# Splitting the first three 256-token passes of an FFN into chunks, with other decode points and lags

## The chip, the cores and the metric

The kernel runs on one core of a Trainium2 chip. The metric is device microseconds of one execution. The core's engines are PE (TensorE, the matrix engine), DVE (VectorE), ACT (ScalarE), POOL (GpSimd) and SP (SyncE, which issues all DMAs here). Each runs its own instructions strictly in the order in which they stand in its stream; semaphores make one engine wait for another.

## The reference, cut to what matters

```python
# q, k, v: (4, 8, 576, 64); windowed causal attention with a distance bias
scores = q @ k.T / 8 + bias, masked to 0 <= i - j < 128
attn   = softmax(scores);  x = (attn @ v)  -> (2304, 512)
x = ((x @ w_a) * (x @ w_b)) @ w_out         # FFN 1: 512 -> 1536 -> 512
h = x @ w_in                                # FFN 2: 512 -> 2048 -> 512
g = where(h >= 1, h, where(h <= -1, 0, (h + 1)**2 / 4))
return g @ w_out2
```

The weights arrive as 64-bit floating point numbers. The kernel turns each 512x128 or 128x512 piece into two 32-bit pieces, `wh` and `wl` (high and low part), and each product of the FFNs is made of three matmuls: `wh*xh`, `wh*xl` and `wl*xh`.

## The kernel before, in words

**Attention.** `attention()` is a generator: every `next` of it (a *step*, made by `step()`) emits one of three things for a round (batch, head pair, pair of 64-query blocks): `scores` (matmuls `ps_s`, L316; bias, mask and row maximum on DVE, L322; exponential on ACT, L326; scaling by the row sum on POOL and ACT), `transposes` (matmuls `ps_t`, L352, of the softmaxed tile `s`), or `values` (matmuls `ps_o`, L377, which use 64 of PE's columns each). The transposes of a round come `LT` = 3 rounds after its scores, its values `LV` = 5 rounds after. A round has one or two *strips*, one DVE instruction L322 each, 144 in all; strips are used as a clock below. In the program's order one `ps_o` instruction is two records of the trace.

**Weights.** `pump()` takes the next weight piece in the order a0, b0, o0, a1, ... (a and b feed the gate of slice f, o its way back), and `decode` emits its load and its conversion: on DVE L471, L474, L475, L476, L478, on ACT L468 and L485, on POOL (for the first 15 pieces) L484 and L142 `wl`. There are 15 slots for pieces, enough for slices 0 to 4, and 2 more once attention is over. A slot comes free when its piece has been used for the last time. Before attention's end pieces are pumped at every second step made while the next half of tokens is being waited for, or when a product asks for a piece that isn't there; the first `HPN` pieces are emitted at high priority.

**FFN 1.** Tokens are cut in nine *halves* of 256 and in five blocks of 512 (the last of 256). While attention runs, FFN 1 goes half by half: for half i and slice f, `gate` makes 24 matmuls into `mm` tiles (L519 to L521, 256 columns wide), then `down1_half` 12 into two `acc` tiles (L592); at the end of a half the `acc` tiles are copied to `y` and written to a DRAM buffer `x2p`. Halves 0 and 1 take slices 0 to 3, the others 0 to 4 (`N0`). After that FFN 1 goes by blocks of 512 columns for slices up to 8 and then up to 11 (`down1`, L620 to L622), starting from what `x2p` holds. FFN 2 follows (L652 to L654). I call all `mm` and `acc` matmuls *FFN matmuls*.

**What sets the order.** `products()` yields after every three matmuls, and each yield earns `PACE` steps of attention (0.8 in the first two halves, then 0.5); before a half begins, steps are made until its tokens are `ready`. The resulting program is then reordered within each engine by a scheduler that works from priorities and its own timeline, so where an instruction stands must be read from the order it made.

Of the kernel before, what the change touches and what calls it, by code (L numbers as in the profile page):

```python
# [9 lines left out]
F32 = mybir.dt.float32  # L10
# [4 lines left out]
ALU = mybir.AluOpType  # L15
# [11 lines left out]
def attention_and_two_ffns(  # L27
# [12 lines left out]
    nc = tc.nc  # L40
# [4 lines left out]
    P = 128  # L45
# [4 lines left out]
    TB = 512  # L50
# [7 lines left out]
    halves = [(t, HB) for t in range(0, NT, HB)]  # L58
# [10 lines left out]
    E_X = ['A', 'A', 'A', 'A', 'A', 'A', 'A', 'A']  # L69
    E_Y = 'AV'  # L70
    G2 = [5, 11]
    HPN = 6
    LORD = [['q', 0, 2, True], ['k', 0, 2, True], ['q', 2, 4, False], ['k', 2, 4, False], ['q', 4, 6, False], ['k', 4, 6, False], ['q', 6, 8, False], ['k', 6, 8, False], ['v', 0, 8, 0]]
    LT = 3
    LV = 5
    N0 = [4, 5, 5, 5, 5]
    N1 = 9
    NDIAG = 2
    PACE = [0.8, 0.8, 0.5, 0.5, 0.5, 0.5, 0.5, 0.5, 0.3]
    PT = 3  # L80
    PUMP = [2, 0]
    SB = 4
    TURN1 = [0, 1, 2, 3, 4]
    TURN2 = [4, 0, 1, 2, 3]
# [21 lines left out]
    later = {}  # L106
# [42 lines left out]
        else:  # L149
            ENG[e].tensor_copy(o, i)  # L150

    count = {"t": 0}

# [245 lines left out]
    done = set()  # L401

    def attention():
        load_start()
        prep_unit(0)
        seen = -1
        for n in range(len(todo) + LV):
            if n < len(todo):
                u, t = todo[n]
                if u != seen:  # L410
                    seen = u
                    if u + 1 < len(units):
                        prep_unit(u + 1)
                    if u + AHEAD < len(units):
                        load_unit(*units[u + AHEAD])
                    values_of[units[u]] = load_values(*units[u])
                scores(*t)
                yield
            if 0 <= n - LT < len(todo):
                transposes(*todo[n - LT][1])  # L420
                yield
            if 0 <= n - LV < len(todo):
                values(*todo[n - LV][1])
                done.add(todo[n - LV][1])
                yield

    def ready(t1):
# [103 lines left out]
    def work(name):  # L531
        if later:
            return later["act"].tile([P, TB], F32, tag="t", name=name)
        return act.tile([P, HB], F32, tag="t", name=name)
# [15 lines left out]

    x2p = dram.tile([P, len(halves), NC, HB], F32, name="x2p")
    sums = {}

    def gate(x, f, n, final):

# [24 lines left out]

    def down1_half(i, f, fs, g, final, accs):

        if f == fs[0]:
            accs[:] = [ps_acc.tile([P, TB], F32, tag="acc", name="acc") for _ in range(2)]
        wh, wl = weight(("o", f))
        gh, gl = (z[:, :HB] for z in g)
        for c in range(NC):
            dst = accs[c // 2][:, (c % 2) * HB : (c % 2) * HB + HB]
            cs = slice(c * P, (c + 1) * P)
            opens, closes = f == fs[0] and c % 2 == 0, f == fs[-1] and c % 2 == 1  # L590
            for z, (w, m) in enumerate(((wh, gh), (wh, gl), (wl, gh))):
                nc.tensor.matmul(  # L592
                    dst, w[:, cs], m, start=opens and z == 0, stop=closes and z == 2,
                    skip_group_check=True,
                )
            yield
        if f in final:
            retired.add(("o", f))
        if f == fs[-1]:
            for z in range(2):  # L600
                y = work("y") if later else act.tile([P, TB], F32, tag="y", name="y", bufs=1)
                ecopy(E_Y[z], y, accs[z])
                nc.sync.dma_start(
                    x2p[:, i, 2 * z : 2 * z + 2, :], y.rearrange("p (c t) -> p c t", c=2)
                )
# [64 lines left out]
    def products():  # L670
        behind = deque()

        def run(up, down, i, fs, x, n, final, lag):
            accs = []
            for f in fs:
                g = yield from up(x, f, n, final)
                behind.append(down(i, f, fs, g, final, accs))
                while len(behind) > lag:
                    yield from behind.popleft()
                if later:  # L680
                    pump()

        turns1 = [
            *((i, range(N0[t0 // TB])) for i, (t0, _) in enumerate(halves)),
            *((i, range(N0[i], N1)) for i in TURN1),
            *((i, range(N1, NF1)) for i in TURN2),
        ]
        last = {f: n for n, (_, fs) in enumerate(turns1) for f in fs}
        for n, (i, fs) in enumerate(turns1):
            final = {f for f in fs if last[f] == n}  # L690
            if fs[0] == 0:
                t0, w = halves[i]
                yield t0 + w
                at = t0 % TB
                x = tuple(z[:, :, at : at + HB] for z in xs[t0 // TB])
                yield from run(gate, down1_half, i, fs, x, w, final, 1)
            else:
                yield from run(gate, down1, i, fs, xs[i], blocks[i][1], final, 1)

        turns = [len(blocks) - 1, *range(len(blocks) - 1)]  # L700
        for fs in groups2:
            if fs[-1] == NF2 - 1:
                turns = range(len(blocks))
            for i in turns:
                final = fs if i == turns[-1] else ()
                yield from run(bend, down2, i, fs, xs[i], blocks[i][1], final, 2)
        while behind:
            yield from behind.popleft()


    at = attention()

    def step():
        if later:
            return
        try:
            next(at)
        except StopIteration:
            first.close()
            later["dec"] = ctx.enter_context(tc.tile_pool(name="wdec2", bufs=1))  # L720
            later["act"] = ctx.enter_context(tc.tile_pool(name="act2", bufs=2))
            later["sum"] = ctx.enter_context(tc.tile_pool(name="sums", bufs=1))
            later["g"] = ctx.enter_context(tc.tile_pool(name="g2", bufs=1))
            w2 = ctx.enter_context(tc.tile_pool(name="w2", bufs=W2))
            later["acc"] = ctx.enter_context(tc.tile_pool(name="ps_acc2", bufs=2, space=PSUM))
            later["mm"] = ctx.enter_context(tc.tile_pool(name="ps_mm2", bufs=2, space=PSUM))
            slots.append((w2, W2, deque()))

    steps = 0
    owed = 0.0  # L730
    begun = -1
    for need in products():
        if need is not None:
            begun += 1
            while not later and not ready(need):
                step()
                steps += 1
                if steps % PUMP[0] == PUMP[1]:
                    pump()
        owed += PACE[min(begun, len(PACE) - 1)]  # L740
        while owed >= 1.0:
            owed -= 1.0
            step()
# [30 lines left out]
```

## Time and profile before

| what | value |
|---|---|
| median of 3 runs | 1011.68 us (1011.15 to 1013.41) |
| profiled execution, whole | 1012.14 us |
| its span in the trace | 1010.0 us |
| PE busy | 985.0 us, 98% of the span |
| DVE busy | 619.2 us, 61% |
| ACT busy | 409.2 us, 41% |
| POOL busy | 184.0 us, 18% |

A busy PE is not PE at its peak: matmuls overlap, and the profile counts the time from one's start to its modelled end. To see PE's true pace, take the distance between the starts of two neighbours. "PEclk" is the share of full clock that PE was granted; the engine knows two levels, 1.2 and 2.4 GHz. Idle time counts only on the engine that sets the end of its stage, so the profile is read by stretches.

### The profile page before, as it was taken

To read this page: it belongs to the slowest core of one execution; us is meant where nothing else is said; L and a number is where in the kernel's file an instruction comes from. 1 tells how busy PE (TensorE), PEld (TensorE's weight loads), DVE (VectorE), ACT (ScalarE), POOL (GpSimd) and SP (SyncE) were. 2 spreads that over 40 slices of the span, in tenths; PEclk is the share of its full clock that TensorE was granted. 3 is DMA by queue.
4 is the path that set the end of the run, shared out by engine and by line. 5 is a ranking of instruction groups with operands and counts; after the bars stand their busy time and mean duration, and the time that the engine had idled before them with its cause. 6 is when DMAs were issued, how large, how long until landed. Compare 5 with 4: busy or idle time off the path is not lost.

```text
span 1010.0 us, 15777 instructions
## 1 busy us (share of the span) xinstructions
PE 985.0 (98%) x5804; PEld 849.7 (84%) x5804; DVE 619.2 (61%) x1393; ACT 409.2 (41%) x975; POOL 184.0 (18%) x300
## 2 busy tenths in 40 slices
PE   5989999999999999999999999999999999999998
PEld 4768899999999988888988888888888888888887
DVE  7999644445437898212897279743996446644443
ACT  5877656565424343111343245433552223322222
POOL 5777522222211100000122224000020000000001
PEclk8999999999999999999999999999999999999999
DMA  7757443243053443000232012200231000001111
GB/s 168 152 126 155 95 91 83 48 81 76 1 188 115 151 152 104 1 1 1 65 104 84 0 42 85 63 1 1 66 102 42 1 1 21 1 1 42 43 42 63
DMA packets 136861, 67.10 MB, mean 66 GB/s; under 512 B 107472, under 2 KB 127952, under 8 KB 136272
## 3 DMA queue, kind: packets, MB, share of 16 engines
q1 hardware_dynamic: 136784, 66.09, 24.4%
q8 instruction: 46, 0.75, 0.3%
q14 instruction: 31, 0.25, 0.1%
HBM read 56.62 MB, written 9.44 MB: 65 GB/s over the span
## 4 chain that ended last, share of the span: by engine, by line
PE 87%; DVE 6%; DMA 3%; ACT 2%; issue 1%; POOL 1%; SPq 1%; DVEq 0%; POOLq 0%; ACTq 0%
PE mm L519 16%; PE mm L520 15%; PE mm L521 15%; PE acc L652 7%; PE acc L653 6%; PE acc L654 6%; PE acc L592 6%; PE ps_s L316 3%; PE ps_o L377 3%; PE acc L622 3%; PE acc L620 3%; PE acc L621 3%; PE ps_t L352 2%; DMA kraw<-in_k_dram 2%; DVE e L478 1%
## 5 line engine op out<-in xcount | busy, mean ns | idle before, releaser
L519 PE MATMUL mm<-xh,wh 128*128 128x512 f32 (+1 forms) x952 | 332.0, 350 | 0.2
L521 PE MATMUL mm<-xh,wl 128*128 128x512 f32 (+1 forms) x952 | 321.0, 337 | 0.9 <-POOL wl L142 0.9
L520 PE MATMUL mm<-xl,wh 128*128 128x512 f32 (+1 forms) x952 | 321.3, 338 | 0.0
L519 PEld LDWEIGHTS mm<-xh,wh 128*128 128x128 f32 x952 | 180.0, 189 | 25.0 <-issue 3.6
L521 PEld LDWEIGHTS mm<-xh,wl 128*128 128x128 f32 x952 | 179.9, 189 | 20.4 <-POOL wl L142 1.1
L520 PEld LDWEIGHTS mm<-xl,wh 128*128 128x128 f32 x952 | 180.0, 189 | 19.7 <-issue 0.3
L575 ACT ACTIVATE c_sb<-c_sb,half 128x512 f32<-128x512 f32 (+1 forms) x80 | 54.5, 682 | 165.7 <-DVE c_sb L574 165.7
L652 PE MATMUL acc<-wh,gh 128*128 128x512 f32 x288 | 112.3, 390 | 0.5 <-ACT gh L541 0.5
L653 PE MATMUL acc<-wl,gh 128*128 128x512 f32 x288 | 112.2, 390 | 0.0
L654 PE MATMUL acc<-wh,gl 128*128 128x512 f32 x288 | 110.4, 390 | 0.0
L574 DVE TENSOR_SCALAR c_sb<-mm 128x512 f32<-128x512 f32 (+1 forms) x80 | 50.8, 635 | 81.8 <-PE mm L521 78.9
L564 DVE TENSOR_TENSOR a_sb<-mm,a_sb 128x256 f32<-128x256 f32 (+1 forms) x79 | 40.5, 513 | 93.8 <-PE mm L521 91.3
L142 POOL TENSOR_TENSOR gl<-c_sb,gh 128x256 fp32r<-128x256 f32 x16 | 15.4, 962 | 384.4 <-ACT gh L541 377.8
L326 ACT ACTIVATE s<-s,nmax 128x192 f32<-128x192 f32 (+2 forms) x144 | 62.1, 432 | 54.2 <-DVE nmax L322 53.1
L142 POOL TENSOR_TENSOR gl<-a_sb,gh 128x256 fp32r<-128x256 f32 x50 | 40.3, 806 | 223.0 <-ACT gh L541 222.7
L576 DVE SCALAR_TENSOR_TENSOR c_sb<-mm,c_sb 128x512 f32<-128x512 f32 (+1 forms) x80 | 50.7, 635 | 39.0 <-ACT c_sb L575 39.0
L322 DVE CUSTOM_DVE_ANT_0 s<-ps_s,bias 128x192 f32<-128x192 f32 (+2 forms) x144 | 43.2, 329 | 47.0 <-PE ps_s L316 46.8
L541 ACT CAST gh<-a_sb 128x256 fp32r<-128x256 f32 (+1 forms) x79 | 38.2, 483 | 83.0 <-DVE a_sb L564 82.8
L541 ACT CAST gh<-c_sb 128x512 fp32r<-128x512 f32 (+1 forms) x80 | 46.2, 579 | 56.3 <-DVE c_sb L576 46.3
L468 ACT ACTIVATE e<-w 128x512 f32<-128x512 f32 x65 | 43.9, 675 | 58.4 <-DMA w<-in_moe_w_out_dram 15.1
L485 ACT CAST wh<-e 128x512 fp32r<-128x512 f32 x68 | 42.2, 621 | 59.3 <-DVE e L484 37.4
L559 ACT COPY a_sb<-mm 128x256 f32<-128x256 f32 (+1 forms) x79 | 35.3, 447 | 75.7 <-PE mm L521 73.1
(83 smaller groups left out, 1672.1 us busy)
## 6 DMA issues: line engine op xcount, KB each, us to landing
w<-in_moe_w_out_dram SPq DMA_DIRECT2D x28, 512.0 KB, 3.5
w<-in_moe_w_in_dram SPq DMA_DIRECT2D x16, 512.0 KB, 3.7
w<-in_moe_w_a_dram SPq DMA_DIRECT2D x12, 512.0 KB, 4.3
w<-in_moe_w_b_dram SPq DMA_DIRECT2D x12, 512.0 KB, 4.2
x2p<-y SPq DMA_DIRECT2D x18, 256.0 KB, 2.1
out_dram<-osum SPq DMA_DIRECT2D x18, 256.0 KB, 2.0
xsum<-x2p SPq DMA_DIRECT2D x4, 1024.0 KB, 6.5
kraw<-in_k_dram SPq DMA_DIRECT2D x64, 56.0 KB, 2.5
```

The source lines that it names most:

```text
L142: eng.tensor_tensor(out_, a, hi.bitcast(F32), ALU.subtract)
L326: nc.scalar.activation(at(z, i), at(z, i), AF.Exp, bias=nmax[:, z : z + 1], scale=-1.0, accum_out=ssum[:, z : z + 1],)
L519: nc.tensor.matmul(ps, wh[:, cs], xh[:, c], start=(c == 0), stop=False)
L520: nc.tensor.matmul(ps, wh[:, cs], xl[:, c], start=False, stop=False)
L521: nc.tensor.matmul(ps, wl[:, cs], xh[:, c], start=False, stop=(c == NC - 1))
L541: nc.scalar.copy(hi[:, :n], t[:, :n])
L574: nc.vector.tensor_scalar(c_sb[:, :n], ph[:, :n], -1.0, None, ALU.max)
L575: nc.scalar.activation(c_sb[:, :n], c_sb[:, :n], AF.Square, bias=half, scale=0.5)
L592: nc.tensor.matmul(dst, w[:, cs], m, start=opens and z == 0, stop=closes and z == 2, skip_group_check=True,)
L652: nc.tensor.matmul(accs[s], gh[:, ss], wh, start=begin, stop=False)
L653: nc.tensor.matmul(accs[s], gh[:, ss], wl, start=False, stop=False)
L654: nc.tensor.matmul(accs[s], gl[:, ss], wh, start=False, stop=end)
```

## The change

Twelve passes over halves take the place of nine: halves 0 and 1 first do slices 0 and 1, half 2 slices 0 to 2; then each returns for the rest up to slice 4. All halves now do slices 0 to 4. A returning pass reads its part of `x2p` back into a tile `before`, adds it on DVE to both `acc` tiles and writes the sum. Pieces are pumped at listed step numbers (`PUMP`: 2, 5, 8, then every sixth step up to 194), whoever makes the step. The first `NEARLY` = 8 rounds have lags 2 and 3 in place of 3 and 5. `PACE` is 0.8 for the first six passes, 0.6 for four, then 0.5. Three pieces, not six, have high priority.

```diff
-    HPN = 6
+    HPN = 3
+    EARLY = (2, 3)
+    NEARLY = 8
-    N0 = [4, 5, 5, 5, 5]
+    N0 = 5
+    HALVES = [[0, 0, 2], [1, 0, 2], [2, 0, 3], [0, 2, 5], [1, 2, 5], [2, 3, 5], [3, 0, 5], ...]
-    PACE = [0.8, 0.8, 0.5, 0.5, 0.5, 0.5, 0.5, 0.5, 0.3]
+    PACE = [0.8, 0.8, 0.8, 0.8, 0.8, 0.8, 0.6, 0.6, 0.6, 0.6, 0.5, 0.5]
-    PUMP = [2, 0]
+    PUMP = [2, 5, 8, 14, 20, 26, 32, ..., 188, 194]
...
+        def lag(n):
+            return EARLY if n < NEARLY else (LT, LV)
+        events = sorted(
+            [(n, 0, n) for n in range(len(todo))]
+            + [(n + lag(n)[0], 1, n) for n in range(len(todo))]
+            + [(n + lag(n)[1], 2, n) for n in range(len(todo))]
+        )
...
         if f == fs[0]:
+            if f > 0:
+                before[i] = (later["sum"] if later else act).tile(
+                    [P, 2, TB], F32, tag="before", name="before", bufs=1
+                )
+                nc.sync.dma_start(
+                    before[i].rearrange("p z (c t) -> p (z c) t", c=2), x2p[:, i]
+                )
...
+                if f >= fs[0] > 0:
+                    y = before[i][:, z]
+                    nc.vector.tensor_tensor(y, accs[z], y, ALU.add)
+                    nc.sync.dma_start(
+                        x2p[:, i, 2 * z : 2 * z + 2, :], y.rearrange("p (c t) -> p c t", c=2)
+                    )
+                    continue
...
+        count["step"] += 1
+        if count["step"] in PUMP:
+            pump()
...
-                steps += 1
-                if steps % PUMP[0] == PUMP[1]:
-                    pump()
```

The first place that matters is PE between strips 52 and 64, where all tokens of batch 0 are done and half 2 is being made ready. Before, half 0 and half 1 stand there (`xh_106` is the high part of the tokens of block 0; `s`, `diag`, `kt`, `v` are tiles of attention):

```order
L520 MATMUL mm<-xl_107,wh 128x256
L521 MATMUL mm<-xh_106,wl 128x256
L316 MATMUL ps_s<-kt,diag_130 128x192 x2
L352 MATMUL ps_t<-ident,s_135 128x128 x4
L377 MATMUL ps_o<-pt,v_150 64x128 x2
L519 MATMUL mm<-xh_106,wh 128x256
L520 MATMUL mm<-xl_107,wh 128x256
L521 MATMUL mm<-xh_106,wl 128x256
```

Now, on PE at the same strips, what stands there is attention and the first matmuls of half 2 (`xh_108` is block 1), taken as its tokens appear:

```order
L319 MATMUL ps_s<-kt,diag_130 128x192 x2
L380 MATMUL ps_o<-pt,v_150 64x128 x4
L355 MATMUL ps_t<-ident,s_138 128x128 x4
L319 MATMUL ps_s<-kt,diag_130 128x192
L530 MATMUL mm<-xh_108,wh 128x256 x2
L531 MATMUL mm<-xl_109,wh 128x256
L532 MATMUL mm<-xh_108,wl 128x256
L531 MATMUL mm<-xl_109,wh 128x256
L532 MATMUL mm<-xh_108,wl 128x256
L355 MATMUL ps_t<-ident,s_141 128x128 x2
```

Counted over the whole order: before strip 52's scores stand 110 FFN matmuls before the change and 120 after it; before strip 64's, 235 and 156; before strip 144's, 1005 and 672. In all there are 4668 and 4704.

The second place is PE after strip 64, where every `ps_o` group stood in one run between FFN matmuls:

```order
L592 MATMUL acc<-gl,wh 128x256
L592 MATMUL acc<-gh,wl 128x256
L377 MATMUL ps_o<-pt,v_150 64x128 x4
L592 MATMUL acc<-gh,wh 128x256
```

With the change, on PE, groups there stand in pieces and next to other attention work:

```order
L612 MATMUL acc<-gl,wh 128x256
L380 MATMUL ps_o<-pt,v_146 64x128 x2
L612 MATMUL acc<-gh,wl 128x256
L380 MATMUL ps_o<-pt,v_146 64x128 x2
L319 MATMUL ps_s<-kt,diag_128 128x192 x2
L355 MATMUL ps_t<-ident,s_138 128x128 x4
L380 MATMUL ps_o<-pt,v_146 64x128 x2
L612 MATMUL acc<-gh,wh 128x256
```

After strip 64, 188 `ps_o` instructions stand in 52 unbroken runs before the change and in 65 after it.

## Rows read from the trace of the kernel before

**Rows 1.** The page: busy time, share and instructions of each engine.

```profile
PE 985.0 (98%) x5804; PEld 849.7 (84%) x5804; DVE 619.2 (61%) x1393; ACT 409.2 (41%) x975; POOL 184.0 (18%) x300
```

**Rows 2.** By stretch: length, busy PE, PEld, DVE, ACT, POOL, clock, DMA share, GB/s.

```profile
10.00:83.20 73.20, 61.47 (x477) 50.64 (x478) 67.92 (x229) 57.79 (x192) 53.77 (x77) 0.95 0.67 144
83.20:112.30 29.10, 28.11 (x225) 24.93 (x222) 25.78 (x72) 18.45 (x56) 18.88 (x26) 1.00 0.67 146
112.30:285.00 172.70, 172.70 (x1490) 158.45 (x1489) 79.73 (x326) 95.70 (x319) 46.48 (x119) 1.00 0.31 65
290.00:340.00 50.00, 50.00 (x419) 50.00 (x419) 32.32 (x58) 18.12 (x40) 8.51 (x11) 1.00 0.49 169
350.00:390.00 40.00, 40.00 (x178) 33.13 (x177) 36.98 (x72) 16.96 (x29) 0.00 (x0) 1.00 0.43 132
```

**Rows 3.** The same view, DVE's instructions on `ps_s` alone: the strips.

```profile
0.00:83.25 83.25, 15.03 (x52) 0.96 0.68 148
83.25:112.35 29.10, 3.85 (x12) 1.00 0.67 146
```

**Rows 4.** The same view, PE on `mm`, then PE on `acc`.

```profile
83.20:112.30 29.10, 13.83 (x90) 1.00 0.67 146
112.30:285.00 172.70, 91.85 (x546) 1.00 0.31 65
...
83.20:112.30 29.10, 5.95 (x36) 1.00 0.67 146
112.30:285.00 172.70, 45.50 (x271) 1.00 0.31 65
```

**Rows 5.** DVE's waits in 83.2:112.3: total, times, longest (0.3 us left out).

```profile
DVE diag L289 <- DMA qraw<-in_q_dram: 1.5, 2, 1.0
DVE ssum L332 <- POOL ssum L331: 1.1, 1, 1.1
```

**Rows 6.** DVE's decode steps by shape in 10:83.2; last row, one of them in 300:600.

```profile
L475 DVE SCALAR_TENSOR_TENSOR up<-w,e 128x512 uint32<-128x512 uint32 x10 | 8.4, 840 | 0.1
L478 DVE SCALAR_TENSOR_TENSOR e<-w,e 128x512 f32<-128x512 uint32 x11 | 7.8, 708 | 0.0
L476 DVE TENSOR_SCALAR e<-up 128x512 uint32<-128x512 uint32 x11 | 7.6, 692 | 0.0
L474 DVE TENSOR_SCALAR e<-e 128x512 uint32<-128x512 uint32 x10 | 7.3, 734 | 0.1
L471 DVE TENSOR_SCALAR e<-e 128x512 f32<-128x512 f32 x10 | 5.5, 548 | 0.2 <-ACT e L468 0.2
...
L474 DVE TENSOR_SCALAR e<-e 128x512 uint32<-128x512 uint32 x33 | 16.4, 498 | 0.1
```

**Rows 7.** PE in order of time, around runs of 8 and of 4 `ps_o` records.

```profile
137.55 0.28 PE L521 MATMUL mm<-xh,wl 128*128 128x256 f32 x1
137.76 0.66 PE L377 MATMUL ps_o<-pt,v 128*64 128x128 f32 x8
...
138.57 0.28 PE L520 MATMUL mm<-xl,wh 128*128 128x256 f32 x1
...
223.19 0.28 PE L592 MATMUL acc<-gh,wl 128*128 128x256 f32 x1
223.40 0.44 PE L377 MATMUL ps_o<-pt,v 128*64 128x128 f32 x4
...
223.99 0.28 PE L592 MATMUL acc<-gl,wh 128*128 128x256 f32 x1
```

**Rows 8.** DVE: the last gate of half 8; later, piece b8 of slice 8.

```profile
342.98 0.42 DVE L564 TENSOR_TENSOR a_sb<-mm,a_sb 128x256 f32<-128x256 f32 x1
...
362.85 0.68 DVE L142 TENSOR_TENSOR wl<-e,wh 128x512 fp32r<-128x512 f32 x1
```

**Rows 9.** PE's longest wait after 10 us, and the stretch around it (columns as Rows 2).

```profile
21.46 0.47 PE L352 MATMUL ps_t<-ident,s 128*128 128x128 f32 x1 [3.18 <-POOL s L337]
...
20.00:30.00 10.00, 8.54 (x51) 6.71 (x52) 8.86 (x29) 6.99 (x25) 6.45 (x9) 0.66 0.69 128
```

## What the change should do to the time

> **What bounds the kernel now.** First the page's busy times [rows 1]: PE is busy all along, DVE for 61%, so what sets the speed must be sought by stretches. Then the busy times by stretch [rows 2], which I cut where strips 52 and 64 are done [rows 3]. From 10 to 83.2 us DVE is busy 67.9 of 73.2 us and PE, with 477 instructions, far below the pace it has later: DVE sets the speed. From 83.2 to 112.3 both are close to full: DVE 25.8, PE 28.1 of 29.1 us. From 112.3 to 285 PE never pauses, while DVE (80 of 173 us) and ACT (96) have room. At 290 to 340 its pace is 419 FFN matmuls of 256 columns in 50 us, 0.119 us each; at 350 to 390, 178 of 512 columns in 40 us, 0.225 us each.
>
> From this follows how to cost the change. After 112 us PE is the bound and its work is nearly fixed, so work that is only moved there gains nothing. What counts is (a) how much PE work is done when the start is over and (b) what is added to PE's work behind that. The bare time to gain is what PE lacks before 112 us.
>
> **The start, up to strip 52.** DVE's order has 11 pieces converted ahead of strip 52 in both versions, one gate product more in the changed one (4 for 3), and 27 for 26 block transposes. `HPN`, `PUMP` and the shorter lags shift single instructions by a few places. I take strip 52 at the same 83.2 us, with 10 more FFN matmuls ahead of it on PE (120 for 110): 10 x 0.119 = 1.2 us to the good. Bounds: DVE idled 5.3 of the 73.2 us, so no more than 5.3 us can be won by better order alone; on the other side, the lag of 2 rounds puts PE behind the softmax of a round sooner, and one more wait like that of 3.18 us, PE for POOL [rows 9], would hold the next scores, for which DVE waits in its turn: 3.2 us lost.
>
> **From strip 52 to 64.** Before, PE makes 125 FFN matmuls here by the order (126 by the trace, 90 + 36 [rows 4]), now 36, because halves 0 and 1 stop after two slices and half 2 has no tokens until strip 62. DVE still converts nearly as many weights: 3 pieces for 4, and 1 gate product for 4. A piece costs DVE 0.84 + 0.71 + 0.69 + 0.73 + 0.55 = 3.5 us [rows 6]; a gate product 0.4 us [rows 8]. That is 3.5 + 3 x 0.4 = 4.7 us less, 25.8 - 4.7 = 21.1 us busy. PE would need 29.1 - 89 x 0.119 = 18.5 us. So DVE sets this stretch. Without waits it takes 21.1 us, with the waits it had here, 2.9 us [rows 5], 24.0; at the share of busy time of the stretch ahead (67.9 of 73.2 us, the nearest row) 22.7, which I take. Strip 64 then comes at 83.2 + 22.7 = 105.9 us, 6.4 us earlier, but with 235 - 156 = 79 FFN matmuls less behind it, 9.4 us of PE's time. Net loss 3.0 us; by the bounds 1.4 to 4.3, and with those of the start -3.9 to 7.5.
>
> The deferred matmuls aren't lost for long, but they are caught up in a stretch where PE is full. From strip 64 on PE has more per strip to do than DVE: to strip 72, 57 FFN matmuls (6.8 us) and four rounds. The stretch from 112.3 us tells a round's price: 172.7 us less 817 FFN matmuls (546 + 271 [rows 4]) x 0.119 leaves 75.5 us for 40 rounds, 1.9 us each. So 14.4 us on PE, against 10.5 on DVE (one piece, 3.5 us, and four rounds of 1.75 us: 79.7 us less some 23 gate products of 0.4 is 70 us for 40).
>
> **From strip 64 to the end of attention.** FFN matmuls per strip fall (516 from here to strip 144, for 770), so attention ends earlier: strip 144 comes at about 105.9 + (516 x 0.119 + 40 x 1.9) = 243 us. That is worth nothing in itself, since PE's work is only put in another order. DVE's 80 and ACT's 96 us of work [rows 2] fit into these 137 us. New is what the order shows: `ps_o` in 65 runs, not 52. A run of eight records between FFN matmuls takes 138.57 - 137.55 = 1.02 us from the last start before to the second start behind, less two paces of 0.119: 0.78 us. A run of four takes 223.99 - 223.19 less the same: 0.56 us [rows 7]. Two runs of four in place of one of eight cost 2 x 0.56 - 0.78 = 0.34 us. 13 more runs: 4.4 us, all on a full PE. Bounds: nothing, if a run beside other attention work starts for free; 6.1 us, if I cost all runs by their sizes (runs of 1 and 2 instructions at 0.56 us, of 3 and 4 at 0.78). The trace's rows have FFN neighbours only, so this is the largest open term; I keep 4.4, since both rows show the price at the run's edges.
>
> The Trainium skill bears on this term: "TensorEngine Tiling (Array Packing)", Key Properties, says that changing the tiling mode drains the engine, whoever the neighbours are. It names no price; by it the extra runs cost wherever they stand, since scores and transposes use the full width as FFN matmuls do.
>
> **Slice 4 of block 0** goes at 256 columns: 72 x 0.119 for 36 x 0.225, 8.57 - 8.10 = 0.5 us more on PE.
>
> **Returning passes.** Six adds of about 0.7 us on DVE (priced as its 512-column steps) lie in PE's stretch, where DVE has 90 us to spare: nothing, unless PE waits for the two `acc` tiles. A pass's first `acc` is needed a whole gate later, 24 matmuls or 2.9 us, so both adds are hidden. Three reads and six writes more pass SP's queue; the read for half 1 waits for the write of half 0 (one `before` tile), and loads of q, k and v queue behind it. These are issued two units of two or three rounds ahead, some 14 us, and the DMA engines are busy 31% there [rows 2]. Nothing.
>
> **Weights at the block turn.** Block 0 now begins with slice 5. Slot rules and DVE's order of decode are the same against half 8's last gate; before, b8 is finished at 363.5 us, 20.6 us after it [rows 8]. PE needs b8 after gates 5, 6 and 7, two ways back and half of gate 8, each gate 24 x 0.225 = 5.4, each way 2.7 us: 16.2 + 5.4 + 2.7 = 24.3 us behind half 8's end. Hidden by 3 or 4 us; if this cover fails, 3 us.
>
> **Sum.** Start +3.0 (the 1.2 us to the good is in the 79 matmuls and isn't taken off again); runs +4.4; slice 4 +0.5. Together 7.9 us. The profiled execution took 1012.1 us, 0.5 above the median; 1011.7 + 7.9 = 1019.6 us.
>
> **Rivals.**
> - *Runs are free beside attention.* 1011.7 + 3.5 = 1015.2 us; with DVE at 21.1 us in strips 52 to 64, 1013.6, within measurement. For it: nothing in the rows but their silence; against it: the price sits at the edges. This and a better start together give "same": 0.16.
> - *DVE's start gets shorter: faster.* A decode step like L474 costs 734 ns at the start and 498 later [rows 6]. If pumping beside attention let all 14 pieces go at the later price, at most 0.24 us on each of about three of five steps, 0.6 us a piece, 8.4 us, and DVE's 5.3 idle us went too, strip 64 would come 13.7 us sooner: 1005.9 us. No change is reached at strip 64 by 98 us, faster by 2 us at 96. Against it: POOL's share of the decode is unmoved in the order, and POOL is busy 53.8 of 73.2 us beside it. 0.16. The skill's "GPSIMD Engine Reference", Specifications, says that POOL shares its way to SBUF with DVE; by it the later price goes with POOL's absence, which the change doesn't bring, so that rule speaks against this rival.
> - *PE waits for attention behind strip 64.* A round comes every 3.4 us, not 4.3; if each of 40 waits 0.25 us, 10 us more: 1030 us. Against it: PE had no wait there, and DVE and ACT are below 70%. 0.05.
> - *PE's clock falls.* After the 3.18 us wait the granted clock was 0.66 over 20 to 30 us [rows 9], so part of it at 1.2 GHz; if the thinner strips 52 to 64 met that, PE's 18.5 us would double past DVE's 22.7 and 14 us be lost: 1034 us. Against it: 10 to 83.2 us is as thin and granted 0.95. 0.03. The skill's "TensorE: Matmul & The Clock Gate", Part 1, has the slow clock as the default that activity lifts; the row agrees.
>
> **How the numbers follow.** My forecast has 0.60: a time of 1019.6, between 1014 and 1025. Below lie "same" (0.16) and "faster" (0.16), above it the last two (0.08). The range for 8 in 10 reaches into "same" and halfway to "faster": 1009 to 1026. A measurement of this kernel tells 0.2%, 2 us, from no change: faster 0.16, same 0.16, slower 0.68.
>
> **What would show it.** Right: strip 64 at 104 to 108 us with about 160 FFN matmuls done; PE without waits from there; `ps_o` runs at 0.56 us and up beside `ps_s` and `ps_t`; strip 144 near 243 us; the first block's pace unbroken. Wrong: strip 64 before 98 us, or runs whose edges cost nothing, or PE waiting for `wl` at the block turn.

## The result and the profile after

The changed kernel takes 1025.45 us (median of 4 runs, 1023.55 to 1026.15) beside 1011.62 for the kernel before: a ratio of 1.013, 95% interval 1.0118 to 1.0142. It is 13.8 us slower; 1019.6 us was forecast. The profiled execution took 1023.55 us, the lowest of the four, with a span of 1021.8 us (1010.0 before): the traces hold 11.8 us of the loss, and 1.9 us lie between this execution and the median. One execution of e10 below took 4639.09 us and is left out of its ratio.

The page's busy times after, beside [rows 1]:

```profile
PE 993.5 (97%) x5840; PEld 854.5 (84%) x5840; DVE 622.0 (61%) x1399; ACT 409.0 (40%) x977; POOL 186.2 (18%) x302
```

By stretch, after, beside [rows 2] (same columns: length, busy PE, PEld, DVE, ACT, POOL, granted clock, DMA share, GB/s), cut where strips 52, 64 and 144 begin:

```profile
10.00:84.90 74.90, 64.09 (x485) 53.27 (x485) 67.64 (x228) 59.05 (x194) 52.14 (x77) 0.93 0.64 142
84.90:106.70 21.80, 17.52 (x135) 14.53 (x135) 21.58 (x61) 16.22 (x49) 15.72 (x23) 0.92 0.72 162
106.70:243.00 136.30, 136.30 (x1128) 118.96 (x1129) 77.12 (x319) 84.97 (x294) 43.59 (x109) 1.00 0.46 97
290.00:340.00 50.00, 50.00 (x419) 50.00 (x418) 6.48 (x14) 10.08 (x26) 8.41 (x12) 1.00 0.12 43
380.00:420.00 40.00, 40.00 (x178) 33.15 (x177) 36.21 (x68) 14.36 (x24) 0.00 (x0) 1.00 0.38 119
```

The strips, after, beside [rows 3] (DVE on `ps_s`; busy time and count):

```profile
0.00:85.30 85.30, 15.14 (x52) 0.94 0.65 146
85.30:107.20 21.90, 3.92 (x12) 0.92 0.72 165
107.20:243.40 136.20, 24.04 (x80) 1.00 0.45 97
```

FFN matmuls on PE, after, `mm` and then `acc`, beside [rows 4]:

```profile
0.00:84.90 84.90, 19.12 (x102) 0.94 0.65 147
84.90:106.70 21.80, 4.20 (x18) 0.92 0.72 162
106.70:243.00 136.30, 55.98 (x338) 1.00 0.46 97
...
0.00:84.90 84.90, 5.32 (x30) 0.94 0.65 147
84.90:106.70 21.80, 2.45 (x14) 0.92 0.72 162
106.70:243.00 136.30, 30.75 (x172) 1.00 0.46 97
```

What the reader is to see: strip 64 comes 5.3 us sooner than before (106.7 for 112.0) with 164 FFN matmuls begun instead of 246; DVE has no gap between strips 52 and 64 (21.58 of 21.8 us), and PE is busy only 17.52 us there; strip 144 comes at 243.0 us, 30.4 sooner than before, with PE never idle between strips 64 and 144.

One number puts such kernels side by side: PE's **account**, the time less 0.119 us for each FFN matmul begun by then. It grows by everything that is not FFN: attention's own work, waits, slow matmuls. The times are those at which the strip begins on DVE, the counts are from the two views just shown. Behind strip 144 I give the rest of the span beside that of before (1010.0 - 153.6 = 856.4 us). The runs of `ps_o` behind strip 64 are those of the instruction order. The last column adds up, over slices of 2 us ahead of strip 64, the slice times one less the granted clock.

| kernel, profiled execution | strip 64 | FFN begun | account at 64 | growth 64 to 144 | rest, beside before | `ps_o` runs | lost clock, us |
|---|---|---|---|---|---|---|---|
| before | 112.0 | 246 | 82.7 | 70.9 | 0 | 52 | 3.4 |
| after | 106.7 | 164 | 87.2 | 75.6 | +2.6 | 65 | 6.8 |
| e1 rates of before | 105.1 | 159 | 86.2 | 71.0 | +0.7 | 52 | 5.1 |
| e2 before, rates of after | 112.3 | 246 | 83.0 | 78.5 | +1.3 | 71 | 3.4 |
| e3 four chunks | 108.8 | 243 | 79.9 | 77.9 | +2.2 | 67 | 0 |
| e4 old lags | 100.2 | 164 | 80.7 | 74.2 | +2.7 | 57 | 0 |
| e5 four chunks, rates | 108.8 | 243 | 79.9 | 71.1 | +2.3 | 52 | 0 |
| e6 rates, old lags | 103.4 | 169 | 83.3 | 71.6 | +3.0 | 51 | 6.8 |
| e7 late weights, rates | 96.1 | 170 | 75.9 | 77.5 | +2.5 | 51 | 0 |
| e8 late weights, rates, lags | 92.3 | 156 | 73.7 | 81.4 | +4.1 | 52 | 3.4 |
| e9 four chunks, rates, lags | 113.0 | 247 | 83.6 | 70.5 | +2.7 | 52 | 6.8 |
| e10 spread weights | 97.3 | 169 | 77.2 | 72.9 | +1.4 | 51 | 1.7 |
| e11 three chunks, spread | 100.9 | 206 | 76.4 | 73.1 | +2.1 | 51 | 1.7 |
| e12 `xl` last | 99.0 | 163 | 79.7 | 70.8 | +3.2 | 51 | 1.7 |

So after stands against before at +4.5 us by strip 64, +4.7 more by strip 144, and +2.6 behind that: 11.8 us. The rows are those of one execution each, which can lie off its kernel's median: after by -1.9 us, e4 -4.2, e6 +2.3, e8 +3.9, e10 -2.8, the others by less than 1. Between strips 64 and 144 PE waits only in e4, e6, e7, e8, e10 and e11; these waits make 1.3, 1.4, 5.6, 4.6, 2.7 and 1.5 us of their growth.

PE's waits at the start, after (total, times, longest), 10 to 112 us:

```profile
PE mm L531 <- DVE xl L145: 5.9, 5, 2.2
PE ps_t L355 <- POOL s L340: 3.2, 5, 1.6
PE ps_t L355 <- DVE ssum L335: 2.1, 1, 2.1
```

The first is new: before had no such line. In order, PE comes to a gate whose tokens' small part `xl` DVE hasn't made yet. What holds DVE up is seen at 88 us, the first lines DVE, then POOL, then PE, all of after in order of time (start, duration, engine, line, tiles; in brackets the wait):

```profile
87.80 1.78 DVE L486 SCALAR_TENSOR_TENSOR up<-w,e 128x512 uint32<-128x512 uint32 x1
89.51 0.34 DVE L325 CUSTOM_DVE_ANT_0 s<-ps_s,bias 128x192 f32<-128x192 f32 x1
...
87.77 1.27 POOL L145 TENSOR_TENSOR wl<-e,wh 128x512 fp32r<-128x512 f32 x1
...
87.81 0.40 PE L530 MATMUL mm<-xh,wh 128*128 128x256 f32 x2
90.28 0.41 PE L355 MATMUL ps_t<-ident,s 128*128 128x128 f32 x2 [2.08 <-DVE ssum L335]
```

DVE's step `up` takes 1.78 us where POOL works on a piece beside it; the mean of the same step in 300 to 600 us is 0.71. PE, with nothing it may do, waits 2.08 us, and in the slices of 2 us behind that wait the granted clock is 0.68, 0.50 and 0.97: part of the time at 1.2 GHz. By longer stretches, after:

```profile
22.00:30.00 8.00, 7.35 (x37) 5.61 (x35) 6.19 (x21) 5.16 (x17) 5.04 (x9) 0.57 0.88 193
42.00:48.00 6.00, 6.00 (x43) 5.10 (x43) 5.90 (x19) 4.68 (x15) 4.62 (x8) 0.72 0.59 144
90.00:96.00 6.00, 5.71 (x38) 5.03 (x38) 6.00 (x20) 5.57 (x19) 4.64 (x7) 0.72 0.61 142
```

The kernel before has the first of these, at 20 to 30 us [rows 9], and not the others.

### The profile page after: what moved, and what is told of

Its sections match the earlier page's. It is cut to its first block, busy times and chain, and to the rows that moved or that the text cites. A ratio compares the mean times of both kernels' runs of the same rounds, so it can differ in the third digit from the quotient of the medians.

```text
span 1021.8 us, 15887 instructions
## 1 busy us (share of the span) xinstructions
PE 993.5 (97%) x5840; PEld 854.5 (84%) x5840; DVE 622.0 (61%) x1399; ACT 409.0 (40%) x977; POOL 186.2 (18%) x302
## 4 chain that ended last, share of the span: by engine, by line
PE 83%; DVE 4%; DMA 2%; issue 1%; ACT 1%; POOL 0%; DVEq 0%; SPq 0%; ACTq 0%; POOLq 0%
PE mm L530 15%; PE mm L531 14%; PE mm L532 14%; PE acc L679 6%; PE acc L680 6%; PE acc L681 6%; PE acc L612 5%; PE ps_o L380 3%; PE ps_s L319 3%; PE acc L648 2%; PE acc L647 2%; PE acc L649 2%; PE ps_t L355 2%; DMA w<-in_moe_w_out_dram 1%; DMA w<-in_moe_w_a_dram 1%
## 5 line engine op out<-in xcount | busy, mean ns | idle before, releaser
L531 PE MATMUL mm<-xl,wh 128*128 128x256 f32 (+1 forms) x960 | 325.2, 339 | 5.9 <-DVE xl L145 5.9
L530 PE MATMUL mm<-xh,wh 128*128 128x256 f32 (+1 forms) x960 | 328.1, 344 | 0.8 <-DVE c_sb L588 0.8
L532 PE MATMUL mm<-xh,wl 128*128 128x256 f32 (+1 forms) x960 | 323.2, 337 | 0.0
L531 PEld LDWEIGHTS mm<-xl,wh 128*128 128x128 f32 x960 | 182.8, 190 | 26.9 <-DVE xl L145 7.1
L532 PEld LDWEIGHTS mm<-xh,wl 128*128 128x128 f32 x960 | 182.7, 190 | 19.0
L679 PE MATMUL acc<-wh,gh 128*128 128x512 f32 x288 | 112.3, 390 | 0.1
L145 POOL TENSOR_TENSOR gl<-a_sb,gh 128x256 fp32r<-128x256 f32 x52 | 43.7, 840 | 255.2 <-ACT gh L552 255.0
L145 DVE TENSOR_TENSOR gl<-c_sb,gh 128x512 fp32r<-128x512 f32 x64 | 44.2, 690 | 32.4 <-ACT gh L552 32.1
```

What stands on the lines that cost most here:

```text
L145: eng.tensor_tensor(out_, a, hi.bitcast(F32), ALU.subtract)
L530: nc.tensor.matmul(ps, wh[:, cs], xh[:, c], start=(c == 0), stop=False)
L531: nc.tensor.matmul(ps, wh[:, cs], xl[:, c], start=False, stop=False)
L532: nc.tensor.matmul(ps, wl[:, cs], xh[:, c], start=False, stop=(c == NC - 1))
L679: nc.tensor.matmul(accs[s], gh[:, ss], wh, start=begin, stop=False)
```

## The experiments

Twelve kernels ran, each beside runs of the kernel before on the same chip (medians 1011.3 to 1011.9). Two rates of attention, two lists of passes and two lags make up most of them. A pass is written as half, first slice, end of slices; "..." stands for the rest of a list, in `HALVES` halves 4 to 8 whole.

### e1: the rates of before

```diff
-    PACE = [0.8, 0.8, 0.8, 0.8, 0.8, 0.8, 0.6, 0.6, 0.6, 0.6, 0.5, 0.5]
+    PACE = [0.8, 0.8, 0.5, 0.5, 0.5, 0.5, 0.5, 0.5, 0.5, 0.5, 0.5, 0.5]
```

> The kernel after with the rates of the kernel before from the third entry of PACE on (0.5 attention steps for each product instead of 0.8 and 0.6). Up to strip 64 the order on PE is that of the kernel after (156 feed-forward matmuls ahead of strip 64's scores); behind it ps_o stands in 52 runs instead of 65. Theory, that each run costs about 0.35 us wherever it stands: 13 runs are 4.4 to 4.8 us, 1020.7 to 1021.1 us beside 1025.5. Rival, that the runs are free and the 4.8 us between strips 64 and 144 came from PE waiting for attention that is asked for too fast: then the gain comes with fewer idle gaps on PE and not with cheaper ps_o blocks. Rival two, that neither costs: 1025.5 within 0.2%.

Measured: 1016.19 us, ratio 1.0051 [1.0036, 1.0066], 9.3 us less than after. Between strips 64 and 144 the account grows by 71.0 us, as before (70.9), instead of 75.6: 4.6 us, what the 13 runs were priced at. It isn't idle time, since neither kernel lets PE pause there. The rest of the gain lies elsewhere: 1.0 us by strip 64 although PE's order is the same up to there, and 1.9 us behind strip 144 (+0.7 for +2.6). So the number that I called the price of the runs holds for its stretch; the medians give twice as much, and the other half is not the runs' by anything seen here.

### e2: the kernel before with the rates of after

```diff
-    PACE = [0.8, 0.8, 0.5, 0.5, 0.5, 0.5, 0.5, 0.5, 0.3]
+    PACE = [0.8, 0.8, 0.8, 0.8, 0.8, 0.8, 0.6, 0.6, 0.5]
```

> The kernel before with the change's PACE cut to nine passes (0.8 six times, 0.6 twice, 0.5): the start up to strip 64 keeps its order but for 9 matmuls behind it, and ps_o stands in 71 runs instead of 52 behind strip 64. Theory, runs at 0.34 us: 19 runs are 6.5 us, 1018.1 us beside 1011.6. Rival, runs free beside the decode: 1011.6 within 0.2%. If earlier attention were worth something by itself, below 1011.

Measured: 1020.55 us, ratio 1.0094 [1.0077, 1.0111], 9.2 us slower. The start is that of before (strip 64 at 112.3 us with 246 matmuls); the growth from 64 to 144 is 78.5 for 70.9 us. Its rows, first `mm`, then `acc`:

```profile
112.30:248.90 136.60, 59.09 (x331) 1.00 0.37 74
...
112.30:248.90 136.60, 26.50 (x159) 1.00 0.37 74
```

136.6 - 490 x 0.119 = 78.3 us for 80 strips (78.5 by whole counts). 7.6 us for 19 runs is 0.40 us each. By the order the runs of `ps_s` and `ps_t` between strips 64 and 144 are as many as before, 45 and 45, and changes of any kind from one group of matmuls to another are fewer (250 for 270). What costs is a change to `ps_o` and back. The rival, that a run is free beside attention, falls. "Earlier attention is worth something" falls too: strip 144 is 24.5 us earlier here and the kernel slower.

How the edges look where attention stands ahead of the run, after, PE in order of time:

```profile
149.60 0.59 PE L319 MATMUL ps_s<-kt,diag 128*128 128x192 f32 x2
150.12 0.44 PE L380 MATMUL ps_o<-pt,v 128*64 128x128 f32 x4
150.49 0.39 PE L612 MATMUL acc<-gh,wh 128*128 128x256 f32 x1
150.72 0.28 PE L612 MATMUL acc<-gl,wh 128*128 128x256 f32 x1
```

Four records of `ps_o` behind `ps_s` take 150.72 - 150.12 = 0.60 us up to the second FFN start behind them; four behind FFN work took 223.99 - 223.40 = 0.59 [rows 7]. The neighbour ahead gives no discount. The Trainium skill, "TensorEngine Tiling (Array Packing)", Key Properties, says that a change of the tiling mode drains the engine; e1 and e2 agree in that one more run cost 0.36 to 0.40 us, a price that the Trainium skill leaves open, while the draining itself shows in no row.

### e3: four chunks first

```diff
-    HALVES = [[0, 0, 2], [1, 0, 2], [2, 0, 3], [0, 2, 5], [1, 2, 5], [2, 3, 5], [3, 0, 5], ...]
+    HALVES = [[0, 0, 4], [1, 0, 4], [2, 0, 5], [0, 4, 5], [1, 4, 5], [3, 0, 5], ...]
```

> The kernel after with HALVES so that the first two halves go through four chunks, the third through all five, and two passes come back: 234 feed-forward matmuls stand ahead of strip 64's scores on PE as in the kernel before (235), instead of 156; ps_o in 67 runs. Theory, that deferring 79 to 82 matmuls past strip 64 cost 3.0 (forecast) to 4.5 us (trace): 1025.5 less that, plus 0.7 us for two more runs, is 1021.7 to 1023.2 us, with strip 64 at 112 us again. Rival, that what was lost at the start is PE's standing in order before matmuls whose tokens come late (waits mm on xl), which goes as well: 2 us more, 1019.7 to 1021. Rival, the start cost nothing: 1025.5.

Measured: 1017.47 us, ratio 1.0066 [1.0051, 1.0081], 8.0 us less than after, more than either theory had. By strip 64 the account is 7.3 us better than after's, and 2.8 better than before's with the same number of matmuls. The growth from 64 to 144 is 77.9 us with 67 runs, 0.47 us for each of 15. Two stretches of its trace, beside after's 0.57 to 0.72 above:

```profile
20.00:30.00 10.00, 6.77 (x52) 5.10 (x49) 9.65 (x33) 8.07 (x29) 6.88 (x11) 1.00 0.80 170
40.00:50.00 10.00, 9.60 (x87) 8.95 (x88) 9.88 (x34) 9.07 (x32) 8.03 (x13) 1.00 0.53 123
```

No slice ahead of strip 64 is below full clock here, and PE's waits for `xl` in front of `mm` are 2.4 us instead of 5.9. So undoing the deferral gives back its 3.9 us (worked out below), and 3.4 us on top, about what the waits for `xl` got shorter. The clock does not show in the times: of e3's four executions the one with a granted clock of 0.997 over the span took 1017.26 us, those with 1.0 took 1017.24 and 1018.24.

### e4: the old lags

```diff
-    EARLY = (2, 3)
+    EARLY = (3, 5)
```

> The kernel after with EARLY = (3, 5), the lags of the later rounds for the first eight too. On PE 108 feed-forward matmuls stand ahead of strip 52 (120 in the kernel after) and 152 instead of 156 ahead of strip 64; ps_o stands in 57 runs instead of 65 behind strip 64. By runs alone: 8 x 0.34 = 2.7 us less, by the four matmuls deferred 0.5 us more: 1023 us. Rival, that the shorter lags brought the first tokens sooner and so shortened PE's waits there: 1026 to 1029 us.

Measured: 1020.0 us, ratio 1.0083 [1.0059, 1.0107], 5.4 us less than after. Its four times reach from 1015.80 to 1021.46, and the profiled one is the lowest: no slice below full clock, strip 64 at 100.2 us with as many matmuls as after, 6.5 us sooner. Both theories are off in their sum. From strip 64 to 144 the growth is 74.2 us for 75.6, but PE waits there, as it doesn't in after:

```profile
PE ps_t L355 <- DVE nmax L325: 1.0, 1, 1.0
PE ps_o L380 <- DVE nmax L325: 0.3, 1, 0.3
```

Without these waits eight runs fewer are 2.7 us, 0.34 each, as the theory had it. That leaves 2.7 us of the 5.4 for the start, where I had put no cost on the shorter lags at all; the 6.5 us of the trace are those of an execution 4.2 us below its median. PE's waits for `xl` in front of `mm`, 10 to 112 us, are 1.4 us.

### e5, e6 and e9: chunks and lags, at the rates of before

e5 (four chunks), e6 (old lags) and e9 (both) stand with e1 as a square. The edit shown is e5's; e6 and e9 also have `EARLY = (3, 5)`, and e6 keeps the change's `HALVES`.

```diff
-    HALVES = [[0, 0, 2], [1, 0, 2], [2, 0, 3], [0, 2, 5], [1, 2, 5], [2, 3, 5], [3, 0, 5], ...]
+    HALVES = [[0, 0, 4], [1, 0, 4], [2, 0, 5], [0, 4, 5], [1, 4, 5], [3, 0, 5], ...]
-    PACE = [0.8, 0.8, 0.8, 0.8, 0.8, 0.8, 0.6, 0.6, 0.6, 0.6, 0.5, 0.5]
+    PACE = [0.8, 0.8, 0.5, 0.5, 0.5, 0.5, 0.5, 0.5, 0.5, 0.5, 0.5]
```

> The kernel after with both the four-chunk passes and the rates of the kernel before (0.8, 0.8, then 0.5): on PE 234 feed-forward matmuls ahead of strip 64, ps_o in 52 runs behind it, 1002 matmuls ahead of strip 144, so all of it as in the kernel before but for slice 4 of block 0 at 256 columns (0.5 us), two returning passes and the short lags of the first eight rounds. Theory, that the deferral and the runs are additive: the kernel with four-chunk passes alone stood at 1017.5 us and lost 7.0 us against the kernel before between strips 64 and 144 with 15 runs more; without these 1010.5 us, within 0.2% of the kernel before. Rival, that the returning passes or the 256 columns cost more behind the attention: 1013 to 1015 us.

> The kernel after with the rates of the kernel before and the old lags (3, 5); the passes of two and three chunks stay. 154 feed-forward matmuls ahead of strip 64, 51 runs of ps_o behind it. What is left of the change at the start is the deferral alone. Theory, that the short lags cost the start 3 to 6 us and that this adds to the runs: 1016.2 less that, 1010 to 1013 us. Rival, that the deferral alone makes the start's loss and the lags nothing: 1016 us with strip 64 at 105 us.

> The fourth corner beside e1, e5 and e6, all with the rates of the kernel before: four-chunk passes and the old lags (3, 5). Of the change only the list of PUMP steps, two returning passes and slice 4 at 256 columns remain; 234 feed-forward matmuls ahead of strip 64, 52 runs of ps_o. With short lags the chunks cost 1016.2 - 1011.7 = 4.5 us, with two- and three-chunk passes the short lags cost 1016.2 - 1013.8 = 2.4 us. Theory, that both add: 1011.7 - 2.4 = 1009.3 us. Rival, that short lags hurt only where the feed-forward work beside them is thin and PE stands before a tokens wait: 1011.7 us.

| median, us (ratio to before) | lags 2, 3 | lags 3, 5 |
|---|---|---|
| passes of 2, 2, 3 chunks | 1016.19 (1.0051 [1.0036, 1.0066]) | 1013.78 (1.0021 [1.0012, 1.003]) |
| passes of 4, 4, 5 chunks | 1011.74 (1.0 [0.9991, 1.0009]) | 1015.66 (1.0038 [1.0023, 1.0053]) |

e5, with both parts undone, is back at the kernel before: the two parts together are the loss. What else the change holds comes to nothing in sum, not in each stretch: e5 is 2.8 us better than before by strip 64 and 2.3 worse behind strip 144. But the square is no sum. Four chunks save 4.5 us with the short lags and cost 1.9 with the old ones; 1009.3 was expected for e9. Its rows, strip 52 to 64, and those of e5:

```profile
79.70:113.00 33.30, 31.86 (x253) 28.28 (x252) 29.96 (x77) 20.27 (x58) 21.64 (x28) 0.99 0.70 147
```

```profile
80.10:108.80 28.70, 27.31 (x225) 24.24 (x223) 26.33 (x73) 18.86 (x57) 20.85 (x27) 1.00 0.70 146
```

e9 makes more of its work here, by the order five pieces for four, and its clock is 0.90 from 10 to 79.7 us where e5's is 1.00. The clock isn't most of it: an execution of e9 with a granted clock of 0.995 over the span took 1016.08 us, one of e5 with 0.996 took 1013.13. The pieces differ as the square does. Counted at the step `e`, L489 on DVE, from 0 us to strip 64, in e1, e6, e5 and e9:

```profile
0.00:105.10 105.10, 10.34 (x14) 0.95 0.67 152
0.00:103.40 103.40, 10.59 (x13) 0.93 0.66 146
0.00:108.80 108.80, 10.98 (x15) 1.00 0.68 152
0.00:113.00 113.00, 10.28 (x15) 0.94 0.66 147
```

With passes of 2, 2 and 3 chunks the old lags leave one piece, 3.5 us of DVE [rows 6], to the time behind strip 64 (e4, too, has 13); with 4, 4 and 5 they only move it from ahead of strip 52 to behind it. So what e4 and e6 gain need not be the lags as such; no run moved the piece alone. Neither chunks nor lags have one price at the start. That they move which steps of DVE and POOL meet, and where PE then stands, is my reading and not shown. The start of one order can't be had by adding those of two others.

### e7 and e8: weights late

```diff
-    PUMP = [2, 5, 8, 14, 20, 26, 32, 38, 44, 50, 56, 62, 68, 74, 80, 86, 92, 98, 104, 110, ...]
+    PUMP = [2, 5, 8, 14, 20, 26, 60, 72, 84, 100, 106, 112, 118, 124, 130]
```

Both are at the rates of before; e8 has `EARLY = (3, 5)` besides.

> The kernel after with the rates of the kernel before, and PUMP so that DVE converts 9 pieces of weights ahead of strip 64 instead of 14 (the two- and three-chunk passes need no more); 166 feed-forward matmuls stand ahead of strip 64. Theory, that DVE sets the speed up to strip 64: five pieces of 3.5 us less, strip 64 near 90 us instead of 105, and since PE has as much done by then, up to 14 us to the good: 1002 to 1006 us beside 1016.2 with the rates alone. Rival, that PE then waits for the later pieces behind strip 64 or for softmax ahead of it: 1010 to 1018 us.

> The kernel with late conversion of weights and the rates of the kernel before, and the old lags (3, 5) besides: 8 pieces converted and 154 feed-forward matmuls on PE ahead of strip 64. Theory, that both gains at the start add: 998 to 1003 us, strip 64 at 86 to 90 us. Rival, that with less for DVE to do the start is set by the softmax chain through ACT and PE, where longer lags give no more: as with late conversion alone.

Measured: 1014.17 us, ratio 1.0028 [1.0018, 1.0037], and 1013.59, ratio 1.0016 [1.0006, 1.0026]. Against e1 that is 2.0 and 2.6 us less; 10 to 14 had been hoped for in e7 and 13 to 18 in e8. The start did what the theory said: strip 64 at 96.1 and 92.3 us, accounts of 75.9 and 73.7 (86.2 in e1). It was then given back: the growth behind is 77.5 and 81.4 us with 51 and 52 runs. e7, strips 64 to 72, to 80, and on:

```profile
96.10:113.30 17.20, 17.20 (x151) 16.04 (x149) 11.09 (x43) 11.63 (x38) 9.31 (x16) 1.00 0.57 137
113.30:130.60 17.30, 15.52 (x131) 13.29 (x129) 15.36 (x42) 10.88 (x33) 12.26 (x15) 1.00 0.78 208
130.60:150.00 19.40, 15.65 (x123) 13.02 (x124) 19.08 (x71) 16.19 (x56) 10.92 (x20) 1.00 0.68 126
```

Where the returning passes ask for their pieces, DVE is full (19.08 of 19.4 us) and PE has gaps. The rival holds: the work was moved to a place where it bounds again.

### e10 and e11: weights spread

Both at the rates of before.

```diff
-    HALVES = [[0, 0, 2], [1, 0, 2], [2, 0, 3], [0, 2, 5], [1, 2, 5], [2, 3, 5], [3, 0, 5], ...]
-    PUMP = [2, 5, 8, 14, 20, 26, 32, 38, 44, 50, 56, 62, 68, 74, 80, 86, 92, 98, 104, 110, ...]
e10:
+    HALVES = [[0, 0, 2], [1, 0, 2], [2, 0, 3], [0, 2, 3], [1, 2, 3], [0, 3, 5], [1, 3, 5], [2, 3, 5], [3, 0, 5], ...]
+    PUMP = [2, 5, 8, 14, 20, 26, 60, 68, 76, 84, 92, 100, 108, 116, 124]
e11:
+    HALVES = [[0, 0, 3], [1, 0, 3], [2, 0, 3], [0, 3, 5], [1, 3, 5], [2, 3, 5], [3, 0, 5], ...]
+    PUMP = [2, 5, 8, 14, 20, 26, 40, 48, 56, 70, 80, 92, 104, 116, 128]
```

> The kernel after with the rates of the kernel before, 6 pieces converted ahead of strip 52 and 10 ahead of strip 64 (11 and 14 in the kernel after), the other five one by one up to strip 84; so that the passes can use them as they come, the first three halves return twice (2, 2, 3 chunks, then 3, 3, then the rest). With late conversion alone strip 64 came with 10 us of the start won, and 7 of them were lost again between strips 72 and 80, where three pieces stood close together and PE was busy 2.48 of 5 us. Theory, that DVE has room for one piece in every two rounds there: the gain stays, 1016.2 - 8 = 1008 us, 1006 to 1010. Rival, that PE loses it elsewhere whatever the spread: 1013 to 1015 us as with late conversion.

> As the kernel with spread conversion, but the first three halves go through three chunks each and come back once for two: 10 pieces ahead of strip 52, 12 ahead of strip 64, 15 at strip 76, and 201 feed-forward matmuls on PE ahead of strip 64 (156 in the kernel after, 235 before). Theory, that both the deferral and DVE's load at the start weigh: between the kernel with four-chunk passes (1011.7) and spread conversion, 1006 to 1011 us. Rival, that the start is set by PE's waits for softmax and tokens, not by DVE's load: 1012 us or more.

Measured: 1012.48 us, ratio 1.0006 [0.9996, 1.0017], and 1010.10 us, ratio 0.9985 [0.9971, 0.9998]. e11 is the one kernel whose interval lies below the kernel before, by 1.5 us: hardly more than can be told from no change. e10 missed its 1006 to 1010 us by its median, though its profiled execution took 1009.66; PE waits there 2.0 us for the add of a returning pass, the one case in which such a pass cost something. In both the account by strip 144 is better than before's (150.1 and 149.5 for 153.6), and 1.4 and 2.1 us of it are gone behind that. e11 from strip 52 to 64:

```profile
79.60:100.90 21.30, 21.30 (x173) 18.36 (x172) 17.95 (x61) 15.75 (x50) 12.72 (x22) 1.00 0.67 147
```

As long as after's 21.8 us, but PE is busy all of it and DVE has 3.3 us free: with pieces spread and three chunks in hand PE, not DVE, sets this stretch.

### e12: products with `xl` last

e1, and in each gate (FFN 2's first product runs through the same lines):

```diff
-            nc.tensor.matmul(ps, wh[:, cs], xh[:, c], start=(c == 0), stop=False)
-            nc.tensor.matmul(ps, wh[:, cs], xl[:, c], start=False, stop=False)
-            nc.tensor.matmul(ps, wl[:, cs], xh[:, c], start=False, stop=(c == NC - 1))
-            yield
+        terms = [(z, xh, c) for c in range(NC) for z in (wh, wl)]
+        terms += [(wh, xl, c) for c in range(NC)]
+        for n, (z, t, c) in enumerate(terms):
+            cs = slice(c * P, (c + 1) * P)
+            nc.tensor.matmul(ps, z[:, cs], t[:, c], start=(n == 0), stop=(n == 3 * NC - 1))
+            if n % 3 == 2:
+                yield
```

> The kernel after with the rates of the kernel before (as e1), and in each gate the four products with xl, the small part of the tokens, behind the eight with xh. In e1 PE stood 6.7 us in front of products with xl in four places ahead of strip 64 (2.3 us at 37.7, 1.4 at 58.6, 3.2 at 96.7), and the granted clock was at 0.5 right behind two of these (60 to 64 us, 100 to 106 us). 155 feed-forward matmuls stand ahead of strip 64 and 51 runs of ps_o behind it, as in e1. Theory, that the start's loss is these waits and the low clock that follows them: waits shorter by about 0.9 us each, no dip behind them, 3 to 5 us to the good, 1011 to 1013 us beside 1016.2. Rival, that PE only waits because DVE sets the start: strip 64 at 105 us again and 1016 us.

Measured: 1011.13 us, ratio 0.9996 [0.9987, 1.0005], 5.1 us less than e1, at the upper end of the theory. e1's wait and clock:

```profile
PE mm L531 <- DVE xl L145: 6.7, 4, 2.9
```

```profile
60.00:64.00 4.00, 3.98 (x26) 3.43 (x27) 3.51 (x9) 2.62 (x8) 3.76 (x5) 0.57 0.66 174
100.00:106.00 6.00, 6.00 (x41) 4.83 (x42) 5.94 (x15) 3.23 (x9) 4.75 (x6) 0.72 0.67 153
```

The same in e12:

```profile
PE mm L532 <- DVE xl L145: 0.6, 1, 0.6
```

```profile
60.00:64.00 4.00, 3.62 (x32) 2.44 (x30) 3.90 (x12) 2.42 (x11) 2.80 (x5) 1.00 0.64 164
79.70:99.00 19.30, 17.63 (x148) 14.30 (x148) 19.14 (x59) 15.51 (x48) 15.66 (x24) 1.00 0.71 160
```

The waits are nearly gone, the low clock behind them is gone, strip 64 comes 6.1 us sooner with as many matmuls begun, and the 6.5 us in the account are still 6.7 at strip 144; 2.5 us are lost again behind it. Not all of it is the waits' doing: by the order 13 instead of 14 pieces stand ahead of strip 64, and DVE is busy 4.8 us less up to there (84.3 us from 10 us on, for 89.0 in e1). The clock can be set apart: at the same granted clock of 0.997 over the span two executions of e1 took 1015.64 and 1016.36 us, two of e12 1011.70 and 1011.88. Waits and the moved piece went together and were not taken apart.

## Where the prediction was right, and where not

**What bounds the stretches: right.** DVE sets strips 52 to 64 (21.58 of 21.8 us busy; 21.1 busy was worked out), PE what lies behind, up to strip 144 without a pause. Strip 144 was put at 243 us and came at 243.0, but that close a hit is luck: the 1.9 us a round were taken from a stretch up to 285 us, past strip 144 (up to it the account of before grows by 70.9 us, 1.77 a round), which is 4.6 us too much in 40 rounds, and the 4.4 us of the runs were left out.

**The sum: too small.** 7.9 us were forecast, 11.8 came in the traces and 13.8 by the medians. That is just above the 1025 us up to which I had given 0.60, and 0.5 us inside the range for 8 in 10. The terms that fell short are the start and what lies behind strip 144.

**Strips 52 to 64: right.** 22.7 us with 36 matmuls was forecast, 21.8 with 32 came; against before that is (126 - 32) x 0.119 - (29.1 - 21.8) = 3.9 us lost, for 4.2.

**The start up to strip 52: the term that was mis-sized.** I took the same time as before and 10 matmuls more, 1.2 us to the good. The account at strip 52 was 69.2 us, 0.6 worse than before's 68.6 (82.9 - 120 x 0.119). e1, with the same order on PE, had 83.1 - 132 x 0.119 = 67.4, the 1.2 us as forecast: executions of one order differ here, and after's had a low clock at 42 to 48 us that e1's hadn't, though that this is the cause is not shown. The start as a whole cost 4.5 us instead of 3.0, inside the wide bounds (-3.9 to 7.5) and just outside the narrow ones (1.4 to 4.3). What I had not priced is the new wait for `xl`, 5.9 us on PE. I had looked at a wait behind the shorter lags, 3.2 us, as a bound, and then taken nothing. In the changed order the longer lags gave back some 2.5 us at the start by the medians (2.7 in e4, 2.4 in e6), with one weight piece less ahead of strip 64; e9 shows that in another order they give nothing.

**The runs of `ps_o`: right, in size too.** 4.4 us forecast, 4.7 by the account, 4.6 back in e1; 0.40, 0.47 and 0.34 us a run in e2, e3 and e4 for 0.34 forecast. The doubt that I kept, neighbours of another kind, is settled.

**Returning passes and the block turn: right.** The six adds take 0.68 us each and PE has no wait for their `acc` tiles; the first block's pace is 178 matmuls in 40 us, as in [rows 2], with no wait for `wl`.

**Behind strip 144: a term that was missing.** I had 0.5 us for slice 4; the trace has 2.6. PE's waits there add up to 1.5 us, for 0.7 before. Two of them, the first near the start of FFN 2:

```profile
636.46 0.50 PE L530 MATMUL mm<-xh,wh 128*128 128x512 f32 x1 [0.77 <-DVE c_sb L588]
...
286.89 0.39 PE L612 MATMUL acc<-gl,wh 128*128 128x256 f32 x1 [0.26 <-POOL gl L145]
```

Nearly every variant has 1.3 to 4.1 us here, whatever its halves, e1 alone 0.7. Slice 4 and the longer waits make 1.3 of the 2.6 us; the rest, in which PE isn't idle, stays open, and so does which order makes the waits.

**The median.** 1.9 us lie between the profiled execution and the median. Where they arise no trace shows, since only one execution of each kernel has one. Low-clock stretches don't account for it: the granted clock over the span is on record for each execution, and after's two with 0.993 took 1023.55 and 1025.19 us, its two with 0.996 took 1025.72 and 1026.15. In e4 time and clock do go together (1015.80 us at 1.0, 1021.46 at 0.992); e6's ten, all at 0.993 to 0.996, range over 3.6 us without it.

**The rivals.** *Runs free* fell with e1 and e2. *DVE's start shorter* fell for the change as it is: strip 64 came at 106.7, not by 98, and DVE's steps beside POOL stayed long. The rule cited against it, the Trainium skill's "GPSIMD Engine Reference", Specifications (POOL shares its way to SBUF with DVE), agrees with the step of 1.78 us. e7, e8, e10 and e11 show that the rival's end is reached by taking pieces out of the start: strip 64 at 92 to 101 us. *PE waits behind strip 64*: none from 106.7 to 243 us. *The clock falls*: it did, in two stretches more than before, but where DVE sets the pace; I had given it 0.03 and the price of a doubled PE time. What it costs by itself no run isolates; e1 and e12 at the same clock, and after's own executions, leave little to it.

## What to carry to other kernels

In a stretch where one engine is full, count its work first, and then ask at which instruction the others will stand in order: here a deferral priced right still came with a start that cost half as much again. Each run of narrow matmuls between wide ones had its price here, 0.34 to 0.47 us, so change how densely work is interleaved only with the number of runs in view. Work taken off a full engine must land where that engine has room, piece by piece, or the gain is given back some strips later.

## What was not expected of the hardware

A DVE step on a 128x512 tile with two inputs that takes 0.71 us on average at 300 to 600 us took 1.78 beside a POOL operation of 1.27 us, so nearly the two in turn. PE's clock fell to 1.2 GHz in or behind waits and came back while PE worked on, but the length of a wait does not tell it: in after a wait of 2.08 us was followed by a granted clock of 0.50, while e3, e4 and e5 kept 1.00 ahead of strip 64 with waits of up to 2.3 us (e4); once, in e8, it fell behind strip 64, with a wait of 2.69 us:

```profile
135.96 0.45 PE L355 MATMUL ps_t<-ident,s 128*128 128x128 f32 x1 [2.69 <-DVE nmax L325]
```

```profile
134.00:142.00 8.00, 6.04 (x29) 4.96 (x30) 6.24 (x22) 4.11 (x14) 4.82 (x8) 0.60 0.66 142
```
